# Banded attention and a GELU feed-forward in one kernel: scores ahead of values where both stand side by side in the second products

## Chip, cores, metric

One core of one Trainium2 chip. In the profile's lines PE is TensorE (matrix products) and PEld its weight loads, ACT is ScalarE, DVE VectorE, POOL GpSimd and SP SyncE. PSUM is the memory, divided into banks, into which the products go. The metric is the device time of one execution in microseconds (us), median of several runs.

The stretch of the trace from the first scores of block 1 to the values of block 7 is "the six blocks".

## The reference

```python
# q, k, v: (8 batches, 8 heads, 576 positions, 64), float32
scores = (q @ k.transpose(0, 1, 3, 2)) / sqrt(64)
scores = where(abs(i - j) <= 32, scores, -1e9)          # a band
attn   = exp(scores - max) / sum
x      = (attn @ v) -> (4608 tokens, 512)               # heads side by side
out    = gelu_tanh(x @ w_in) @ w_out                    # 512 -> 2048 -> 512
```

## The kernel before

All products are fp16 with fp32 accumulation. The 4608 tokens are taken in nine blocks of 512. In each block the first products (x by w_in, GELU) come before the second products (by w_out, in a seven-product scheme: 112 products of 128 x 128 by 256 columns). Among the second products of block t stands the attention of batch t + 1, in steps, at positions that a plan names:

```python
PLAN = {6: "s0 v-1", 24: "s1", 26: "m0", 31: "x-1", 40: "m1", 42: "v0 s2", 48: "x0", 56: "m2",
        61: "v1 s3", 64: "x1", 80: "m3", 81: "v2 s4", 88: "x2", 97: "v3", 104: "m4", 112: "x3"}
```

Groups 0 to 3 are pairs of heads; group 4 is the tail of the sequence (written -1 in the next block). The steps, cut:

```python
ap_ = tc.tile_pool(name="ap_", bufs=2)                  # two buffers for each tag
psS, psO = ...                                          # PSUM, one buffer for each tag

def score(b, g):                                        # "s"
    for hf, (m, prs, pieces) in enumerate(halves_of(b, g)):
        ps = psS.tile([128, 2, 512], FP32, name="ps_s", tag=f"S{hf}")
        ...                                             # 4 products on TensorE, keys by queries
        pe = ap_.tile([128, 2, w], FP16, name="pe", tag=f"pe{hf}") if g < 4 else \
            tailp.tile([128, 2, w], FP16, name="pet")
        nc.scalar.activation(pe, ps[:, :, 0:w], AF.Exp, scale=SCALE)

def mask(b, g, hfs=(0, 1)): ...                         # "m": pe times a 0/1 band, on DVE

def weigh(b, g, other=False):                           # "v"
    o = psO.tile([128, 512], FP32, name="ps_o", tag="O")
    d = psO.tile([128, 512], FP32, name="ps_d", tag="D")
    ...                                                 # 8 products with V into o, 8 with ones into d

def invert(b, g, d):                                    # belongs to "v"
    nc.scalar.activation(lt, d, AF.Ln)
    nc.scalar.activation(lt, lt, AF.Exp, scale=-1.0)

def spread(b, g, o, lt):                                # "x": xT = o times lt, on DVE
    nc.vector.tensor_tensor(xT[...], o[...], lt[...], op=ALU.mult)
```

`xT` is a ring of 1536 columns; in blocks 1 and 4 the 480 columns of a spread wrap, and the spread is two instructions.

The softmax here doesn't subtract the row's maximum and nothing guards it: scores larger than these inputs give would overflow.

Of the kernel before, what the change touches and what calls it, by code (L numbers as in the profile page):

```python
# [33 lines left out]
def width(pieces):  # L34
# [7 lines left out]
        ("S1", "T1", True), ("A22", "T4", False), ("S4", "B22", False)]  # L42


PLAN = {6: "s0 v-1", 24: "s1", 26: "m0", 31: "x-1", 40: "m1", 42: "v0 s2", 48: "x0", 56: "m2",
        61: "v1 s3", 64: "x1", 80: "m3", 81: "v2 s4", 88: "x2", 97: "v3", 104: "m4", 112: "x3"}



# [12 lines left out]
def kernel(  # L62
# [366 lines left out]
    def ffn_in(t, n, d0=0, d1=4, then=True):  # L429
        fc = column(t, n)  # L430
        if n == 0 and d0 == 0:
            gTs[t] = gp.tile([128, NF, 512], FP16, name="gT", tag="gT")
        if d0 == 0:
            if t == 0 and 2 <= fc < 6:
                if fc % 2 == 0:
                    phs["S"] = psS.tile([128, 2, 512], FP32, name="ph2", tag=f"S{fc // 2 - 1}")
                phs[fc] = phs["S"][:, fc % 2, :]
            else:
                if t:
                    i = (first(t), 2, 1 - first(t))[n % 3] if n < NF - 1 else 2  # L440
                else:
                    i = fc if fc < 2 else (fc - 4) % 3
                phs[fc] = bank(i) if i < 2 else psO.tile([128, 512], FP32, name="ph", tag="D")
        ph = phs[fc]
        for dc in range(d0, d1):
            nc.tensor.matmul(ph, w_in16[:, dc, fc * 128:fc * 128 + 128],  # L446
                             xT[:, dc, t * 512 % RING:t * 512 % RING + 512],
                             start=(dc == 0), stop=(dc == 3))
        if d1 == 4 and then:
            gelu(t, n)  # L450
# [246 lines left out]
    for t in range(NT):  # L697
        b = t + 1
        att = b < B
        if t:  # L700
# [4 lines left out]
            for fc in range(begun, NF):  # L705
                ffn_in(t, fc)
        plan = PLAN_0 if not t else PLAN if att else {6: "v-1", 31: "x-1"} if t == B - 1 else {}

# [85 lines left out]
```

## Time and profile before

| | before |
|---|---|
| median | 311.4 us |
| span of the profiled run | 310.0 us |
| start-up, to the first scores of block 1 | 75.5 us |
| the six blocks | 191.35 us |
| rest, from the values of block 7 | 43.1 us |
| waits of TensorE at values, over the six blocks | 0.53 us |

The three stretches add up to the span. The last row counts what goes beyond the 0.20 us that the first values take to follow a full-width product even when nothing is waited for. The lines that carry this stand in the prediction. Besides them, the page's group of the values' weight loads (count | busy, mean ns | idle before them and what ended most of it):

```profile
L387 PEld LDWEIGHTS <-V 128*64 128x64 f16 x336 | 18.1, 109 | 12.0 <-issue 5.7
```

"issue" is time for which the profile shows nothing that was waited for. From block 1 on it is 17 times that same gap, about 0.20 us where values follow a full-width product, 3.6 us in all; the other 2.1 of the 5.7 us lie in the start-up.

### The profile page before, as it was taken

Reading aid. Unit: us, or ns where it says so; the run is one execution under the profiler, and the core shown is the slowest. Engines: PE = TensorE matmul, PEld = TensorE weight load, DVE = VectorE, ACT = ScalarE, POOL = GpSimd, SP = SyncE. Lnnn points to the kernel's source line nnn. Section 1 sums busy time; section 2 is a strip of 40 time slices with the busy share of each in tenths; the row PEclk is TensorE's granted clock in tenths of the full one; section 3 lists DMA queues with packets and bytes.
Section 4 is the critical chain, followed back from the end, with each engine's and each line's share of the span. In section 5 each row is a group of like instructions: output and inputs, shape, how many; then the busy total and the mean of one; then the engine's idle time right before and its main releaser. Section 6 shows DMA issues by size and latency. Waiting matters only on the chain.

```text
span 310.0 us, 6731 instructions
## 1 busy us (share of the span) xinstructions
PE 298.4 (96%) x2643; PEld 187.5 (61%) x2643; DVE 198.4 (64%) x453; ACT 200.1 (65%) x315; POOL 104.1 (34%) x158
## 2 busy tenths in 40 slices
PE   7879999999999999999999999999999999999993
PEld 3453545445784588548854785478647764784583
DVE  5663587768969477947785678666866643633451
ACT  1676576567677786768676777677768676706600
POOL 3656456093019210921094108510710061006000
PEclk9999999999999999999999999999999999999999
DMA  6999998999987998799779995999391022004013
GB/s 198 247 333 373 373 348 164 316 191 152 227 178 177 158 216 128 137 173 242 131 157 138 258 132 126 167 223 165 90 170 34 2 69 68 2 0 135 2 37 99
DMA packets 120061, 50.64 MB, mean 163 GB/s; under 512 B 101327, under 2 KB 113359, under 8 KB 120030
## 3 DMA queue, kind: packets, MB, share of 16 engines
q1 hardware_dynamic: 84329, 37.50, 57.2%
q0 software_dynamic: 34768, 11.54, 31.4%
q10 hardware_dynamic: 933, 1.18, 1.2%
q8 instruction: 20, 0.33, 0.5%
q14 instruction: 11, 0.09, 0.1%
HBM read 37.62 MB, written 9.44 MB: 152 GB/s over the span
## 4 chain that ended last, share of the span: by engine, by line
PE 78%; SPq 10%; DMA 7%; DVE 2%; issue 1%; POOL 0%; POOLq 0%
PE mm L544 31%; PE mm L446 22%; PE ph L446 13%; SPq L139 5%; PE ps_o L387 4%; PE ps_s L354 3%; DMA wst<-in_moe_w_in_dram 3%; PE ps_d L387 3%; DMA qr<-in_q_dram 3%; SPq L130 2%; DMA tr<-in_k_dram 1%; PE mm L515 1%; SPq L181 1%; SPq L143 1%; SPq L185 1%
## 5 line engine op out<-in xcount | busy, mean ns | idle before, releaser
L446 PEld LDWEIGHTS <-w_in 128*128 128x128 f16 x576 | 56.0, 98 | 66.4 <-POOL w_in L190 1.1
L446 PE MATMUL mm<-xT,w_in 128*128 128x512 f16 x352 | 86.3, 379 | 0.6 <-DVE xT L411 0.6
L506 POOL DMA_DIRECT2D out_dram<-y x77 | 45.2, 595 | 115.4 <-DVE y L573 114.7
L454 ACT ACTIVATE gT<-mm 128x512 f16<-128x512 f32 x88 | 52.4, 599 | 37.1 <-PE mm L446 37.1
L446 PE MATMUL ph<-xT,w_in 128*128 128x512 f16 x224 | 58.6, 379 | 0.2 <-POOL w_in L190 0.2
L490 DVE TENSOR_TENSOR s<-gT 128x512 f16<-128x512 f16 x64 | 26.9, 420 | 42.1 <-ACT gT L454 42.1
L544 PEld LDWEIGHTS <-s 128*128 128x128 f16 x512 | 48.6, 98 | 7.5
L360 ACT ACTIVATE pe<-ps_s 128x704 f16<-128x704 f32 x64 | 43.3, 728 | 8.8 <-PE ps_s L354 8.8
L544 PE MATMUL mm<-t,s 128*128 128x256 f16 x376 | 45.7, 273 | 0.0
L401 ACT ACTIVATE lt<-ps_d 128x480 f32<-128x480 f32 (+3 forms) x40 | 22.2, 556 | 31.1 <-PE ps_d L387 31.1
L454 ACT ACTIVATE gT<-ph 128x512 f16<-128x512 f32 x56 | 33.0, 599 | 13.0 <-PE ph L446 12.9
L544 PEld LDWEIGHTS <-gT 128*128 128x128 f16 x384 | 36.0, 98 | 7.3
L544 PE MATMUL mm<-w_out,gT 128*128 128x256 f16 x256 | 32.8, 273 | 0.0
L369 DVE TENSOR_TENSOR pe<-pe,mask 128x704 f16<-128x704 f16 x64 | 31.5, 528 | 1.9 <-ACT pe L360 1.7
L411 DVE TENSOR_TENSOR xT<-ps_o,lt 128x480 f16<-128x480 f32 (+5 forms) x38 | 20.2, 548 | 12.5 <-ACT lt L402 12.5
L387 PEld LDWEIGHTS <-V 128*64 128x64 f16 x336 | 18.1, 109 | 12.0 <-issue 5.7
L402 ACT ACTIVATE lt<-lt 128x480 f32<-128x480 f32 (+3 forms) x40 | 23.5, 587 | 1.3
L387 PE MATMUL ps_o<-pe,V 128*64 128x160 f16 (+2 forms) x244 | 21.8, 241 | 1.1 <-POOL V L263 0.8
L87 ACT ACT_TABLE_LOAD x17 | 21.8, 1283 | 1.1 <-PEq L778 0.8
L387 PE MATMUL ps_d<-pe,ones 128*64 128x192 f16 (+2 forms) x264 | 22.4, 235 | 0.0
L170 POOL DMA_DIRECT2D V<-in_v_dram x24 | 22.0, 942 | 0.0
L387 PEld LDWEIGHTS <-ones 128*64 128x64 f16 x336 | 18.6, 110 | 0.1
(77 smaller groups left out, 298.1 us busy)
## 6 DMA issues: line engine op xcount, KB each, us to landing
kr<-in_k_dram SPq DMA_DIRECT2D x32, 256.0 KB, 6.3
qr<-in_q_dram SPq DMA_DIRECT2D x6, 1024.0 KB, 7.3
V<-in_v_dram POOLq DMA_DIRECT2D x30, 128.0 KB, 8.0
wst<-in_moe_w_in_dram SPq DMA_DIRECT2D x3, 1024.0 KB, 7.9
wst<-in_moe_w_out_dram SPq DMA_DIRECT2D x3, 1024.0 KB
qr<-in_q_dram SPq DMA_DIRECT2D x8, 256.0 KB
vr<-in_v_dram SPq DMA_DIRECT2D x16, 128.0 KB, 7.6
out_dram<-y POOLq DMA_DIRECT2D x24, 48.0 KB, 2.4
```

Of the source, the lines that this page charges most:

```text
L87: nc.scalar.add_instruction(mybir.InstLoadActFuncSet(name=nc.get_next_instruction_name(), act_func_set_id=which, ins=[], outs=[]))
L170: nc.gpsimd.dma_start(V[:, c, :, :], v[b, :, 128 * c:128 * c + 128, :].rearrange("h p d -> p h d"))
L360: nc.scalar.activation(pe, ps[:, :, 0:w], AF.Exp, scale=SCALE)
L369: nc.vector.tensor_tensor(pe, pe, m.rearrange("p (o w) -> p o w", o=1).broadcast_to(list(pe.shape)), op=ALU.mult)
L387: nc.tensor.matmul(bk[r0:r0 + 64, at:at + 4 * n].rearrange("d (j p) -> d j p", j=4)[:, :, p0 - q0:p1 - q0], V[:, c, 2 * pr + h, :] if w == ...
L401: nc.scalar.activation(lt[:, 0:n], d[:, 0:n], AF.Ln)
L402: nc.scalar.activation(lt[:, 0:n], lt[:, 0:n], AF.Exp, scale=-1.0)
L446: nc.tensor.matmul(ph, w_in16[:, dc, fc * 128:fc * 128 + 128], xT[:, dc, t * 512 % RING:t * 512 % RING + 512], start=(dc == 0), stop=(dc = ...
L454: nc.scalar.activation(gTs[t][:, fc, :], phs[fc], AF.Gelu_apprx_tanh)
L490: nc.vector.tensor_tensor(dst, x, y, op=op)
L506: (eng or turn_about[0] if t == NT - 1 else eng or nc.gpsimd).dma_start(out_v[b, j, q0 + p:q0 + p + e, cols], yo[m:m + e, cols])
L544: nc.tensor.matmul(pys["apart"][:, 0:256] if apart else py[:, blk, :], lhsT, wino[w][:, f, :], start=(new and i % (8 if one else 16) == 0) ...
```

## The change

Its intent: where values of one group and scores of a later one stand at the same place, issue the scores first, so that they reach ACT and DVE sooner and cover a wait that the values might have.

```diff
-PLAN = {..., 42: "v0 s2", 48: "x0", 56: "m2",
-        61: "v1 s3", 64: "x1", 80: "m3", 81: "v2 s4", 88: "x2", ...}
+PLAN = {..., 42: "s2 v0", 48: "x0", 56: "m2",
+        61: "s3 v1", 64: "x1", 80: "m3", 81: "s4 v2", 88: "x2", ...}
```

No instruction is added. The orders of TensorE and ACT change, those of DVE, GpSimd and SyncE do not.

More of the change, by code (lines that the diff above doesn't have):

```diff
@@ L42 @@
         ("S1", "T1", True), ("A22", "T4", False), ("S4", "B22", False)]
-PLAN = {6: "s0 v-1", 24: "s1", 26: "m0", 31: "x-1", 40: "m1", 42: "v0 s2", 48: "x0", 56: "m2",
-        61: "v1 s3", 64: "x1", 80: "m3", 81: "v2 s4", 88: "x2", 97: "v3", 104: "m4", 112: "x3"}
+PLAN = {6: "s0 v-1", 24: "s1", 26: "m0", 31: "x-1", 40: "m1", 42: "s2 v0", 48: "x0", 56: "m2",
+        61: "s3 v1", 64: "x1", 80: "m3", 81: "s4 v2", 88: "x2", 97: "v3", 104: "m4", 112: "x3"}
 TURN_0 = {10: 0, 12: 1, 14: 2, 15: 3}
```

## The prediction

> **What bounds the kernel now.** I read the page's busy shares first, then the chain that ended last, then the busy time by stretch, and last the timeline of one stretch.
>
> ```profile
> PE 298.4 (96%) x2643; PEld 187.5 (61%) x2643; DVE 198.4 (64%) x453; ACT 200.1 (65%) x315; POOL 104.1 (34%) x158
> PE 78%; SPq 10%; DMA 7%; DVE 2%; issue 1%; POOL 0%; POOLq 0%
> ...
> 74.89:106.30 31.41, 31.05 (x293) 20.42 (x292) 24.23 (x57) 22.78 (x36) 11.18 (x16) 1.00 1.31 183
> 106.30:138.10 31.80, 31.80 (x297) 20.81 (x296) 21.98 (x51) 23.38 (x37) 11.20 (x16) 1.00 1.22 165
> 138.10:169.90 31.80, 31.80 (x297) 20.83 (x296) 22.00 (x51) 23.38 (x37) 11.18 (x16) 1.00 1.15 166
> ```
>
> The first line is the page's busy time, the second the chain's share by engine. The other three are stretches with their length, then the busy time of PE, weight loads, DVE, ACT and POOL, then the clock. TensorE is busy for all 31.80 us of a 31.80 us stretch at full clock. So nothing that gives DVE, ACT or a queue more room can shorten a stretch: only fewer or shorter TensorE gaps can, and every new gap there is paid in full. There are six such stretches with the changed plan (token blocks 1 to 6). In each, 112 second products are interleaved with scores (s), masks (m), values (v: products with V and, for the denominator, with ones) and spreads (x: output times inverse denominator).
>
> The timeline of the third stretch, from values 0 to values 1 (start, length, engine, line, what):
>
> ```profile
> 144.57 0.92 DVE L369 TENSOR_TENSOR pe<-pe,mask 128x704 f16<-128x704 f16 x2
> 144.94 0.26 PE L387 MATMUL ps_o<-pe,V 128*64 128x160 f16 x2
> ...
> 145.65 0.47 PE L354 MATMUL ps_s<-QT,KT 64*128 64x160 f16 x8
> 145.76 0.57 ACT L401 ACTIVATE lt<-ps_d 128x480 f32<-128x480 f32 x1 [1.32 <-PE ps_d L387]
> 146.04 0.83 PE L544 MATMUL mm<-w_out,gT 128*128 128x256 f16 x6
> 146.36 0.60 ACT L402 ACTIVATE lt<-lt 128x480 f32<-128x480 f32 x1
> 146.71 1.58 PE L544 MATMUL mm<-t,s 128*128 128x256 f16 x13
> 146.87 1.33 ACT L360 ACTIVATE pe<-ps_s 128x704 f16<-128x704 f32 x2
> 146.91 0.69 DVE L559 COPY y<-mm 128x512 f32<-128x512 f32 x1 [1.43 <-PE mm L544]
> 147.52 0.65 DVE L411 TENSOR_TENSOR xT<-ps_o,lt 128x480 f16<-128x480 f32 x1
> 148.22 0.11 PEld L387 LDWEIGHTS <-V 128*64 128x64 f16 x2 [0.21 <-DVE xT L411]
> 148.22 0.26 PE L387 MATMUL ps_o<-pe,V 128*64 128x160 f16 x2
> ```
>
> The reader is to see the ring: values 0 end, ACT takes the logarithm of the denominator and the exponential of its negative, DVE spreads the output, and only then may values 1 start, because there is one bank for the output (tag O, one buffer). The spread ends at 148.17 and values 1 start at 148.22, after the ordinary 0.20 us that follows a full-width product. The ring closes with no slack to speak of.
>
> **What the Trainium skill says.** "PSUM — Partial Sum Buffer", section Engine vs sequencer instructions: the queues of ScalarE, VectorE and GpSimd are strict first-in first-out, and matmuls start and complete in program order. The trace agrees: the exponentials of scores 2 start at 146.87, behind the two steps of values 0, though scores 2 were finished near 146.1. "Perfetto Trace Analysis", section Optimization Strategy: the same gap repeating on the engine that should be saturated can mean too few buffers for the next tile. In this trace that gap is all but absent (0.06 us in block 4 and 0.43 us in block 1, below); I expect the change to create it. "TensorE: Matmul & The Clock Gate", section The mechanism: a weight load is pulled ahead of running matmuls if it does not conflict with them. Here a full-width product is followed by another after 0.109 us and by the first scores or values after 0.20 us, so a change of tiling costs about 0.1 us; the change leaves the number of such changes as it was.
>
> **The change part by part.** No instruction is added or removed, and DVE, POOL and SP keep their order; on PE and ACT blocks are swapped at three places in each of six blocks.
>
> (a) TensorE's own time. Before: product to values 0.20, values to scores 0.70, scores to product 0.40 us. After: product to scores 0.20, scores to values 0.39 (the pair "scores 0, values -1" already stands so, 139.55 to 139.94), values to product 0.70 (154.44 to 155.14). Sums 1.30 and 1.29: worth nothing.
>
> (b) ACT's order. Exponentials of the scores (two instructions) now stand ahead of the logarithm of the values. Worse, score tiles after exp and mask (pe) have two buffers for each half. Scores 2 reuse the buffer of group 0, scores 3 that of group 1, and those are read by the very values that now follow. The wait lists of the two built programs agree: before, these exponentials wait for their own scores; after, the first waits for the last product of the values' first half, the second for the last of the second half, and the logarithm waits for nothing more. Scores are early on TensorE, but their exponentials are not early on ACT.
>
> (c) The new ring, from the start of one values block to the next permitted start: first half read 0.494 after the start (product starts at +0.248, lasts 0.246); semaphore 0.042 (same as from the last denominator product to the logarithm); first exponential to second 0.654 (the spacing after an idle ACT, as at 45.5 us of the span; 0.638 where ACT runs on); second to logarithm 0.584 (same place); logarithm to exponential 0.609; to spread 0.636 (as 153.02 to 153.66); spread 0.66 from idle; spread's end to the values' start 0.055 (84.559 to 84.614 in block 1). Sum 3.734 us.
> TensorE gets from values 0 to values 1 in 0.703 + 2.178 (19 products) + 0.395 (scores 3) = 3.276: stall 0.458. From values 1 to values 2 in 0.703 + 2.288 (20 products) + 0.277 (scores 4) = 3.268: stall 0.466.
>
> (d) Values 2 to values 3. Scores 4 have their own tile, so their exponential need not wait: it fits before values 2 end. Ring: 0.813 (values' start to logarithm, 151.609 to 152.422) + 0.602 + 0.636 + 0.66 + 0.055 = 2.766. Before, scores 4 lay between: 0.703 + 0.277 + 1.851 = 2.831, so no stall. Now they lie ahead: 0.703 + 1.851 = 2.554, stall 0.212. This one needs no shared score buffer; the output bank alone makes it.
>
> (e) Sum. In blocks 2, 3, 5 and 6: 0.458 + 0.466 + 0.212 = 1.136 us. In blocks 1 and 4 the ring xT wraps within the 480 columns, the spread is two instructions and 0.062 us longer: 1.322. Against it goes what these two wait already: block 4, 0.062; block 1, 0.428 at values 1 (DVE is behind with weight differences there) and 0.041 at values 0. So 4 x 1.136 + (1.322 - 0.062) + (1.322 - 0.469) = 4.54 + 1.26 + 0.85 = 6.66 us. All on the path, as TensorE never idles elsewhere in these stretches. 311.4 + 6.65 = 318.0 us, 2.1% longer.
>
> **The rivals.** *The intent: earlier scores feed masks and values sooner, and scores fill time in which values wait for a spread.* For it: block 1 really waits 0.43 us at values 1, and scores do not need the output bank. Against it: the whole of such waits over six blocks is 0.53 us, and masks are never waited for in these blocks. If the exponentials did not have to wait for the values (were the buffers enough), the first could start 0.37 us after the scores do (0.325 to the end of their first half, 0.042 for the semaphore), which is 0.02 before the values' start instead of 0.54 after it. The ring would be 0.56 us shorter, 3.17, and only the stall of 0.2 at values 3 would be left: about 312.2 us.
> *Only the swap on TensorE counts; all waits fit.* Then 311.4, with nothing to gain by (a). Against it speaks the slack of nil at 148.17 to 148.22: anything put ahead of the logarithm moves the spread.
> *The delays add up through DVE:* a later spread pushes masks 2 and 3 and the evictions behind it, DVE's order being fixed. By my arithmetic mask 2 ends about 0.8 us after values 1 start, long before values 2; the eviction at product 79 starts about 0.1 us before values 2 start and is needed only by product 96. So no further stall; if I am wrong, another 0.1 to 0.3 us per block, 319 to 320 us.
>
> **Range and chances.** The sum is eighteen stalls of 0.2 to 0.5 us, each the difference of two numbers near 3 us known to about 0.02 to 0.04. A common error of 0.04 gives 0.7 us; missed waits on DVE add up to 1; a spacing of 0.638 rather than 0.654 takes off 0.2. I predict 318.0, range 316.6 to 319.2. The line of 2% lies at 317.6, inside the range and just under the middle: slower by over 2% has 0.59, within 2% 0.40, faster 0.01, as no term shortens TensorE's path.
>
> **What would show it.** In the changed trace, TensorE's wait at the values' line for the spread (DVE, L411) should grow from 2.2 us to about 8 on the weight loads (values 1 and 2, each gap counted with its ordinary 0.2), with some 1.4 more on the products of values 3; the first exponential of scores 2 and 3 should start about 0.54 us after the first product of the values, and the logarithm 1.24 after that; each of blocks 2, 3, 5, 6 should last 32.9 instead of 31.8 us; values 3 should wait about 0.2, with no exponential of scores at fault. If the exponentials start before the values' first half is read, step (b) is wrong; if values 3 wait while values 1 and 2 do not, only (d) was right and the time is near 312.5; if blocks 1 and 4 lose as much as the others, the credit for their present waits was wrong.

## The result, and the profile after

| | before | after |
|---|---|---|
| median of four runs | 311.42 us | 319.05 us |
| span of the profiled run | 310.0 | 316.8 |
| start-up, to the first scores of block 1 | 75.47 | 75.81 |
| the six blocks | 191.35 | 197.95 |
| rest | 43.14 | 43.08 |

The ratio is 1.0249 (95% interval 1.0228 to 1.0269): slower. A ratio is the mean time of one kernel's fast runs over that of the other's of the same rounds, so it is not quite the quotient of the medians. Executions over 1.5% slower than the fastest of the same kernel are left out of the means. The six blocks carry 6.60 us of the 6.87 by which the two traces differ.

Busy time and chain, as in the prediction:

```profile
PE 300.0 (95%) x2643; PEld 188.1 (59%) x2643; DVE 198.8 (63%) x453; ACT 200.8 (63%) x315; POOL 102.2 (32%) x158
...
PE 68%; ACT 9%; DMA 7%; DVE 5%; SPq 5%; issue 4%; POOL 1%; POOLq 0%
```

TensorE's busy time is nearly the same while its share of the chain fell from 78 to 68%. ACT, which had no entry in the list before, has 9%, and DVE went from 2 to 5%: they now stand between one piece of TensorE's work and the next. The stretch that corresponds to the 31.80 us ones (length, then busy time of PE, weight loads, DVE, ACT, POOL):

```profile
108.17:141.10 32.93, 32.02 (x297) 20.94 (x296) 21.98 (x51) 23.50 (x37) 11.20 (x16) 1.00 1.20 161
141.10:174.03 32.93, 32.01 (x297) 20.93 (x296) 21.99 (x51) 23.50 (x37) 11.17 (x16) 1.00 1.07 164
```

The stretch is 1.13 us longer, and TensorE idles for 0.91 of it. (The other 0.22 us are counted as busy, I take it because the modelled tail of the last product reaches into each pause. The pauses beyond the ordinary gaps add up to 1.13.) The timeline from values 0 to values 1 in block 3:

```profile
147.25 0.46 PE L354 MATMUL ps_s<-QT,KT 64*128 64x160 f16 x8
...
147.64 0.26 PE L387 MATMUL ps_o<-pe,V 128*64 128x160 f16 x2
...
147.89 0.25 PE L387 MATMUL ps_d<-pe,ones 128*64 128x192 f16 x2
...
148.18 1.35 ACT L360 ACTIVATE pe<-ps_s 128x704 f16<-128x704 f32 x2 [1.44 <-PE ps_d L387]
...
149.42 0.58 ACT L401 ACTIVATE lt<-ps_d 128x480 f32<-128x480 f32 x1
150.02 0.60 ACT L402 ACTIVATE lt<-lt 128x480 f32<-128x480 f32 x1
150.52 0.27 PEld L354 LDWEIGHTS <-KT 64*128 64x128 f16 x8 [0.21 <-issue]
...
150.66 0.66 DVE L411 TENSOR_TENSOR xT<-ps_o,lt 128x480 f16<-128x480 f32 x1 [0.76 <-ACT lt L402]
...
151.37 0.11 PEld L387 LDWEIGHTS <-V 128*64 128x64 f16 x2 [0.58 <-DVE xT L411]
151.37 0.26 PE L387 MATMUL ps_o<-pe,V 128*64 128x160 f16 x2 [0.38 <-DVE xT L411]
```

Scores 2 begin at 147.25, but ACT stands idle until 148.18, and what ends its 1.44 us of idleness is a denominator product (ps_d), not a score: the exponential waits for the values' products that still read the buffer it is to overwrite. The logarithm of those values, before at 0.81 us after their start, comes at 1.78. The spread ends at 151.32 and values 1 start at 151.37. The ring is 3.73 us long. At values 3 of the same block:

```profile
157.15 0.66 DVE L411 TENSOR_TENSOR xT<-ps_o,lt 128x480 f16<-128x480 f32 x1 [0.68 <-ACT lt L402]
...
157.46 0.27 PE L544 MATMUL mm<-w_out,s 128*128 128x256 f16 x1
...
157.87 0.26 PE L387 MATMUL ps_o<-pe,V 128*64 128x160 f16 x2
```

After the product at 157.46 the values would start 0.20 us later, at 157.66; the spread ends at 157.81 and they start at 157.87, 0.21 us late. The page's two groups on the values' line:

```profile
L387 PEld LDWEIGHTS <-V 128*64 128x64 f16 x336 | 18.7, 109 | 15.8 <-DVE xT L411 8.0
L387 PE MATMUL ps_o<-pe,V 128*64 128x160 f16 (+2 forms) x244 | 21.8, 241 | 6.6 <-DVE xT L411 5.3
```

The waits for the spread are now the largest at these loads, 8.0 us. (A stalled load and its product are both counted.)

### The profile page after: what moved, and what is told of

It reads as the page before. It is cut to its first block, busy times and chain, and to the rows that moved or that the text cites. A ratio compares the mean times of both kernels' runs of the same rounds, so it can differ in the third digit from the quotient of the medians.

```text
span 316.8 us, 6713 instructions
## 1 busy us (share of the span) xinstructions
PE 300.0 (95%) x2643; PEld 188.1 (59%) x2643; DVE 198.8 (63%) x453; ACT 200.8 (63%) x315; POOL 102.2 (32%) x158
## 4 chain that ended last, share of the span: by engine, by line
PE 68%; ACT 9%; DMA 7%; DVE 5%; SPq 5%; issue 4%; POOL 1%; POOLq 0%
PE mm L446 22%; PE mm L544 20%; PE ph L446 13%; PE ps_o L387 4%; DVE xT L411 4%; PE mm L515 4%; ACT lt L402 3%; DMA wst<-in_moe_w_in_dram 3%; DMA wst<-in_moe_w_out_dram 3%; ACT lt L401 3%; ACT pe L360 3%; PE ps_s L354 3%; PE ps_d L387 3%; SPq L130 2%; SPq L139 1%
## 5 line engine op out<-in xcount | busy, mean ns | idle before, releaser
L87 ACT ACT_TABLE_LOAD x17 | 21.8, 1283 | 1.1 <-PEq L778 0.8
L354 PE MATMUL ps_s<-QT,KT 64*128 64x192 f16 (+5 forms) x336 | 17.9, 227 | 1.1 <-DVE KT L290 1.1
```

Source lines behind the costliest of these rows:

```text
L354: nc.tensor.matmul(ps[:, h, off:off + 4 * n].rearrange("k (j p) -> k j p", j=4), KTs[b % 2][r0:r0 + 64, pr, k0:k0 + 128], QTs[b][r0:r0 + 6 ...
```

## The experiments

The theory: TensorE's order costs nothing by itself. The stalls at values 1 and 2 come from ACT's order together with the two buffers of masked scores (an exponential that must wait for the values is queued ahead of the logarithm on which the next values depend). The stall at values 3 comes from the output bank alone. Rivals: the cost lies in TensorE's own change of order; the exponentials cost by standing ahead of the logarithm, whatever they wait for; the waits hang together, so that what is saved at one place comes back at another.

In the expectations, "six blocks" is counted from the first product of block 1, which is 0.75 us before its first scores when these need not wait. In several runs they did wait there, for a transposed key tile from the start-up (up to 1.8 us), so the table below starts at the scores, and the expected numbers have 0.75 taken off.

| run | median us | before | ratio (95%) | six blocks expected | six blocks measured |
|---|---|---|---|---|---|
| before | | | | | 191.35 |
| after_again | 318.49 | 312.02 | 1.0213 (1.0189 to 1.0238) | 197.95 | 197.95 |
| only42 | 316.65 | 312.02 | 1.0154 (1.0131 to 1.0177) | 196.05 | 196.04 |
| only61 | 315.99 | 312.02 | 1.0132 (1.0112 to 1.0153) | 195.45 | 195.84 |
| only81 | 312.92 | 312.02 | 1.0042 (1.0017 to 1.0067) | 192.75 | 192.73 |
| bufs3 | 312.74 | 311.36 | 1.0036 (1.0014 to 1.0057) | 192.35 | 192.26 |
| split3 | 314.64 | 311.36 | 1.0099 (1.0075 to 1.0123) | 192.25 | 193.84 |
| split2 | 312.96 | 311.36 | 1.0052 (1.0026 to 1.0077) | 190.85 | 192.46 |
| v3late | 317.91 | 311.36 | 1.0202 (1.0176 to 1.0228) | 196.6 | 196.68 |
| split2late | 313.24, one run | 311.17 | none | 191.55 | 191.53 |
| best_a | 311.12 | 311.17 | 0.9999 (0.9964 to 1.0033) | 190.95 | 190.87 |
| best_b | 311.41 | 311.17 | 1.0002 (0.9974 to 1.0030) | 190.85 | 190.86 |

All gave the right result. Kernels are compared only within the same rounds. Against the line of 2%, after_again and v3late are unclear and the other runs of several rounds are the same as the kernel before, so the argument below rests on the six blocks. For only42 to only81 the expected column is 191.35 plus the loss expected. The start-up ran from 74.8 to 76.9 us over these traces.

### after_again: the change once more

> The changed kernel unaltered. Its first trace accounts for 6.60 us in the six blocks (from the first values of block 1 to those of block 7) and 0.33 in the start-up, but the medians differ by 7.6. If the six blocks alone make the difference, this run's blocks again show +6.6 and the rest is spread of the start-up, so that the difference of the medians may come out anywhere from 6.6 to 7.7. If something else in the change costs 0.7 us, it should show as the same stretch being longer in both traces of the changed kernel.

The six blocks repeat at 197.95; the medians now differ by 6.5 us instead of 7.6. The extra 1 us of the first comparison is not in the blocks. The start-up's spread is large enough for it, and the start-up is the same program in both kernels; that it lies there is not shown.

### only42, only61, only81: one pair at a time

```diff
 only42:  42: "s2 v0"   61: "v1 s3"   81: "v2 s4"
 only61:  42: "v0 s2"   61: "s3 v1"   81: "v2 s4"
 only81:  42: "v0 s2"   61: "v1 s3"   81: "s4 v2"
```

> Only scores 2 before values 0; the other two pairs as before. Theory (the ring through the shared score buffers): values 1 now come 0.40 us sooner after values 0, because scores 3 do not lie between, so the stall per block is 3.734 - 2.881 = 0.85 us, in all 4 x 0.85 + (0.915 - 0.469) + (0.915 - 0.062) = 4.7 us: 316.1, and no stall at values 2 or 3. Rival (each swap costs the same by itself, a third of the whole): about 314.

> Only scores 3 before values 1. Theory: values 2 follow after 0.703 + 2.288 = 2.991 us while the ring takes 3.734, a stall of 0.74 per block at values 2; block 1 gains 0.40 because its late spread is now covered by scores 3. In all about 4.1 us: 315.5. Rival (a third each): about 314.

> Only scores 4 before values 2. Their exponential has a tile of its own and need not wait for values. Theory: a stall of 0.21 (0.27 in blocks 1 and 4) at values 3 alone, as scores 4 no longer lie between values 2 and 3: 1.4 us, 312.8. Rival (a third each): about 314. Rival (the score buffers are the whole cause): 311.4.

Waits beyond the ordinary gap, per block, in blocks without the wrap: only42 0.85 at values 1 and none later; only61 0.74 at values 2 alone; only81 0.21 at values 3 alone. These are the expected numbers. only61 missed by 0.4 us, all in block 1: values 0 waited 0.42 there for an earlier spread, against 0.04 in the kernel before. That trace had the shortest start-up: TensorE began block 1 0.70 us earlier than in the kernel before, while the spread in question started only 0.33 us earlier (79.88 against 80.21). So TensorE met a DVE that was still behind; that the short start-up is the cause is argued, not tried.

The three losses are 4.7, 4.5 and 1.4 us, 10.6 in all (10.2 without those 0.4), while the three pairs together lose 6.6. The pairs help each other: with all three swapped, the scores of the next pair stand in front of the values that wait and cover 0.40 us (at values 1) or 0.28 us (at values 2) of the ring.

That only81 loses anything speaks against the score buffers as the whole cause. No run gave the values a second output bank, so that this bank is what holds values 3 is read from the trace above and not shown by an experiment.

### bufs3: the wait for the buffer taken away, ACT's order kept

```diff
-pe = ap_.tile([128, 2, w], FP16, name="pe", tag=f"pe{hf}") if g < 4 else \
+pe = yp.tile([128, 2, w], FP16, name="pe", tag="yo") if b > 1 and g == 2 else \
+     ap_.tile([128, 2, w], FP16, name="pe", tag=f"pe{hf}") if g < 4 else \
```

Three plain buffers do not fit (the build refuses them); the pool `yp` is unused after the first block, and its memory goes to group 2, so that scores 2 and 3 no longer overwrite what the values after them read.

> The changed order, but the masked scores of group 2 have tiles of their own (memory that is free after the first block), so that no exponential of scores waits for values. ACT's order stays that of the change. Theory (shared score buffers make the stalls at values 1 and 2): the ring shrinks from 3.73 to 3.17 us, under TensorE's 3.27, so no wait at values 1 and 2 outside block 1; values 3 still wait 0.21 (0.27 with the wrap). Six blocks 193.1 us against 198.7 of the changed kernel and 192.1 of the one before; about 312.4 at the median. Rival (the exponentials' place ahead of the logarithm costs by itself, whatever they wait for): waits of 0.4 us stay at values 1 and 2, 316 to 318.

Block 3 again, from scores 2 to the spread:

```profile
145.17 0.46 PE L354 MATMUL ps_s<-QT,KT 64*128 64x160 f16 x8
145.54 1.35 ACT L361 ACTIVATE pe<-ps_s 128x704 f16<-128x704 f32 x2 [0.88 <-PE ps_s L354]
...
145.56 0.26 PE L388 MATMUL ps_o<-pe,V 128*64 128x160 f16 x2
...
146.77 0.58 ACT L402 ACTIVATE lt<-ps_d 128x480 f32<-128x480 f32 x1
147.38 0.60 ACT L403 ACTIVATE lt<-lt 128x480 f32<-128x480 f32 x1
...
148.02 0.66 DVE L412 TENSOR_TENSOR xT<-ps_o,lt 128x480 f16<-128x480 f32 x1 [0.19 <-ACT lt L403]
```

Now a score (ps_s) releases the exponential, at 145.54, just before the values start. The logarithm comes 1.21 us after that start (1.78 in the change), the spread ends at 148.68, and values 1 do not wait. The waits left are 0.07 at values 1 of block 1, and 0.21 or 0.27 at values 3 in every block. ACT's order is that of the change, so the order alone, without the wait for the buffer, does not make the stalls at values 1 and 2.

### split3 and split2: TensorE's order kept, ACT's put back

```diff
-42: "s2 v0"              61: "s3 v1"              81: "s4 v2"
+42: "p2 v0 e2"           61: "p3 v1 e3"           81: "p4 v2 e4"     # split3
+42: "p2 v0 e2"           61: "p3 v1 e3"           81: "v2 s4"        # split2
```

p is the scores' products, e their exponentials; v contains the logarithm and the exponential of its negative.

> TensorE's order is that of the change at all three places, ACT's order that of the kernel before: the products of the scores come ahead of the values, their exponentials after the logarithm and its exponential. Theory: TensorE's order costs nothing by itself, so values 1 and 2 do not wait (block 1 at most 0.1); only values 3 wait, 0.21, or less by nothing, since that stall comes from the output bank. Six blocks 193.0, about 312.3. Rival (the switch from scores to values on TensorE is what costs): as slow as the change, 318.5.

> As the previous one, with values 2 ahead of scores 4 as before. Theory: no waits but 0.1 at values 1 of block 1, where the kernel before has 0.43, and none in block 4: six blocks 191.6, half a microsecond under the kernel before; about 311.3 at the median, which five rounds may just fail to tell from the kernel before.

The waits at values went as expected: none at values 1 and 2 in any block, and at values 3 0.21 (0.27 with the wrap) in split3 and none in split2. Both runs missed all the same, by 0.27 us in each block. In split2 the pause stands in the middle of scores 3:

```profile
146.99 1.33 ACT L371 ACTIVATE pe<-ps_s 128x704 f16<-128x704 f32 x2
...
147.95 0.18 PEld L354 LDWEIGHTS <-KT 64*128 64x128 f16 x5 [0.21 <-issue]
147.95 0.74 PE L354 MATMUL ps_s<-QT,KT 64*128 64x160 f16 x8
148.38 0.11 PEld L354 LDWEIGHTS <-KT 64*128 64x128 f16 x3 [0.25 <-issue]
```

The eight products take 0.74 us instead of 0.46. The profile calls the pause "issue", but the second half of the scores has one bank, and the exponential that reads it ends at 148.32; the next weight load follows at 148.38. I had checked the values' ring and forgotten the scores' own: by issuing scores 3 sooner and the exponentials of scores 2 no sooner, I had closed it. That is read from these two times and tried next.

### split2late: is it that bank?

```diff
-61: "p3 v1 e3", 64: "x1",
+64: "p3 v1 e3", 67: "x1",
```

> The kernel with the exponentials put back behind the logarithm lost 0.27 us in each block where nothing was expected: the second half of scores 3 waits, I now think, for the one score bank of that half, which the late exponential of scores 2 still reads (its end 148.32, the next weight load 148.38). Theory: with scores 3 and values 1 three products later (64 in place of 61, 0.33 us) the pause inside scores 3 is gone; values 2, now three products nearer to values 1, wait 0.10 (0.16 with the wrap) for the spread. Six blocks 192.3 us against 193.2. Rival (a cost of the split itself, such as the later exponentials delaying masks): the 0.27 stays, 193.2 or more.

One run and one trace. The pause in scores 3 is gone, values 2 wait 0.10 (0.16 with the wrap), and the six blocks take 191.53. That fits the bank, and the rival (a cost of the split itself) falls; no run gave that half a second bank. The sum also closes: 191.35 of the kernel before, less its waits of 0.53, plus 0.71 of waits here, is 191.53. The order of TensorE, swapped here at two of the three places, costs nothing by itself.

### v3late: do the waits hang together?

```diff
-97: "v3"
+99: "v3"
```

> The changed kernel with values 3 two products later (99 in place of 97). Theory: these two products (0.218 us) take up the stall at values 3 (0.21; in blocks 1 and 4 0.27 becomes 0.05), values 1 and 2 wait as in the change: six blocks 197.3 to 197.4, about 317.2. Rival (the waits hang together and what is saved at one values block comes back at the next): as the change, 198.7.

Values 3 wait 0.05 in blocks 1 and 4 and nothing elsewhere; values 1 and 2 wait as in the change (0.45 and 0.46, with the wrap 0.52 and 0.53). The six blocks fall by 1.27 us, and nothing comes back later.

### best_a and best_b: the 0.53 us that the kernel before waits

```diff
 best_a: bufs3 with   97: "v3"            ->  100: "v3"
 best_b: before with  61: "v1 s3", 64: "x1"  ->  65: "v1 s3", 68: "x1"
```

> The change with tiles of their own for group 2 and values 3 three products later (100 in place of 97). Theory: no wait at any values block but 0.07 in block 1: six blocks 191.7 us, under the 192.1 of the kernel before. At the median about 0.4 us less than before, inside the spread of the start-up.

> The kernel before, its order kept (values 1, then scores 3), with this pair four products later (65 in place of 61) and spread 1 after it (68). Theory: the four products (0.44 us) cover the late spread of blocks 1 and 4, and nothing else moves onto TensorE's path, as values 2 still come 2.95 us after values 1 and the ring of the kernel before needs 2.77 to 2.83: six blocks 191.6 us. At the median about 0.5 us less than before. Rival (the intent of the change is needed for that): 192.1.

Both take 0.5 us off the six blocks in the trace, 190.87 and 190.86 against 191.35. In the time this isn't seen: the ratios are 0.9999 and 1.0002, each with 1 in its interval. best_b needs no swap and no buffer, so the intent of the change is not needed for what it could have won.

## Why the prediction was right

The predicted time was 318.0 in a range of 316.6 to 319.2; the median is 319.05, in the repeat 318.49. Slower by over 2% was given 0.59. The first comparison says so clearly (1.0249), the repeat leaves it open (1.0213, interval from 1.0189).

- *TensorE bounds the six blocks, every gap is paid.* Right. Stall for stall, the waits add up to what the blocks grew by.
- *(a) The swap itself is worth nothing.* Right: scores to values 0.39, values to product 0.70; split3 and split2, with TensorE's order swapped, have no wait at values 1 or 2; in split2late the sum closes without any cost of the swap.
- *(b) The exponentials wait for the values through the shared buffers.* Right: the releaser in the trace is the denominator product, at +0.54 us as said, and the logarithm follows 1.24 later. bufs3 takes just this wait away and 5.69 of the 6.60 us with it.
- *(c) The ring.* 3.734 predicted; 3.730 and 3.732 measured. Stalls at values 1 and 2: 0.458 and 0.466 predicted, 0.455 and 0.464 measured (0.52 and 0.53 with the wrap).
- *(d) Values 3.* 0.212 predicted, 0.207 measured, and it is independent of the score buffers (bufs3 keeps it, only81 shows it by itself).
- *(e) The sum.* 6.66 predicted, 6.60 measured in the trace. The sum was right to 1% (block 1 lost 0.85 and block 4 1.26, as said). The median came out 1 us above the middle, 0.15 under the upper end of the range, and that 1 us is not in the blocks. What the prediction left out is that the constant part is not constant: 0.33 us of start-up between the two traces, and a difference of medians of 7.6 in one comparison and 6.5 in the next. The range allowed for errors of the ring and of DVE and not for this spread, so that the first median still fell inside it is in part luck.
- *The rivals.* The intent (earlier scores fill waits) would by the prediction's own arithmetic have given about 312.2 with enough buffers. bufs3 is that kernel, and it gave 312.74, 0.91 us over the kernel before in the trace; even then it does not win, because values 3 lose more than block 1 gains. The pile-up through DVE had 319 to 320 us, and the first median lies there, but it did not occur: the waits at the values alone make up the 6.60 us, and v3late shows them to be separate.
- *A slip.* The weight loads of values 1 and 2 were to wait about 8 us for the spread, and the page has 8.0. But 7.0 of it stands at values 1 and 2, and 1.0 at values 3 of blocks 1 and 4; I had counted an ordinary 0.2 in each gap, and after scores it is 0.13. That the figure agrees is luck. Of the products I said that 1.4 us would show at values 3; the page has 5.3, of which 4.9 stand at values 1 and 2, because a stalled weight load leaves its product idle as well, and the profile counts both.

## What to carry to other kernels

Where an in-order engine serves two chains, moving one chain's step ahead on another engine also moves it ahead in that queue, if the two are issued together; look up which buffer the step writes, since a reader that comes later than before turns the move into a wait in front of the other chain. Write each ring as a sum of measured pieces and compare it with the time in which the bound engine comes round; do this for every single-buffered bank, not only for the one in question (split3 and split2 missed by one forgotten bank). And when a difference is below the spread of the start-up, read it from the repeating stretch of the trace.

## What the Trainium skill lacked or had wrong

- "TensorE: Matmul & The Clock Gate", section Back-to-back issue gap, gives about 131 ns per matmul of 512 columns as the sustained rate of a stream of weight load and matmul pairs, and says that its formula of 216 ns over-counts there. Here 64 such pairs take 13.81 us, 216 ns each at full clock (and 109 ns for 256 columns): the formula holds, the 131 ns does not.
- "ScalarE: Activation LUTs", section What ACT_TABLE_LOAD costs, gives about 1283 ns for the load and about 1380 ns more for a drain, about 2.66 us for every change of table set. The load is as stated: the 17 here take 1.28 us each. The drain does not show: in block 3 of the kernel before, 1.31 us pass from the end of the last GELU (139.60) to the start of the first exponential (140.91).
- "Perfetto Trace Analysis", section Optimization Strategy, says that repeating bubbles can mean too few buffers. bufs3 agrees (5.69 us). What the passage lacks is the order of issue: both kernels have the same buffers, the bubbles came with the order, and v3late took 1.27 us of them off with no buffer added.
- No page that I read gives the time from the end of a product or an elementwise instruction to the start of the one that it releases on another engine. Here it was 0.055 us from a DVE end to the weight load it releases, and 0.042 from a matmul's modelled end to the activation.
